# Attention and a two-layer expert on one core: a written table of one line per expert step takes the place of per-step lists

## The chip, the cores and the metric

The kernel runs on one core of one Trainium2 chip. The metric is the device time of one execution in microseconds. The profile is of one execution on the same core, with a record of each instruction, each DMA packet and the TensorE clock that was granted.

The engines are named as in the profile: PE is TensorE's matmul, PEld its weight load, DVE is VectorE, ACT is ScalarE, POOL is GpSimd and SP is SyncE. Each engine carries out its own instructions in the order in which the program issues them, and waits on semaphores for what the other engines give. So the order in which the Python program calls its functions sets the order of every engine's list.

## The reference

Eight batches of eight heads (576 positions, 64 values a head) go through causal attention with a window of 128 and a bias that falls with distance. The result, 4608 tokens of 512 values, goes through a two-layer expert with an ELU.

```
scores = scale * (q @ k^T);  rel = i - j
scores = where((rel >= 0) & (rel < 128), scores - slope[h] * abs(rel), -1e9)
x = (softmax(scores) @ v), heads side by side        # 4608 x 512
h = x @ w_in                                         # 4608 x 2048
g = where(h > 0, h, exp(min(h, 0)) - 1)
out = g @ w_out                                      # 4608 x 512
```

## The kernel before, in words

The expert sets the beat. Its first layer, `hidden`, works in steps: 512 columns of one PSUM bank each, that is four chunks of 128 features by 128 tokens (or eight by 64) in the first 1024 tokens, and two chunks by 256 tokens from token 1024 on (16 steps for each 512 tokens). A step is 16 matmuls (32 where the tokens lie over the end of the ring `xT`, which holds three batches), about 0.87 us on PE. From step 24 on the two banks `hp[0]` and `hp[1]` take turns.

The ELU of a step is a chain over engines. In a "soft" step (the set `SOFT`) ACT does a Relu (L312) and an Exp (L313). In the others ACT does one Exp (L315) and POOL clips it (L316). Then DVE forms `g` from that and the bank (`elu`, L323). The bank is free after that, so step s+2 cannot start on PE before `elu` of step s is done on DVE.

The second layer works for most tokens in units of 256 tokens by a seven-product scheme: `sums` makes four sums of blocks of `g` on DVE (tiles `S1` to `S4`), `product` runs seven products of 8 matmuls each, in the order 1, 2, 6, 5, 7, 3, 4. They take turns in two banks: 1, 6, 7 and 4 in one, 2, 5 and 3 in the other (`op` and `av`, which change roles from unit to unit). Products accumulate on what is in the bank, so ACT copies the bank out between them (tile `U`, or the output tile after product 4: L396, L398), and DVE's `combine` ("C11", "C12", "C22") reads banks and copies and writes the output tile. A bank is written again only when the copy or the combination that reads it is done.

The attention of batches 2 to 7 runs beside this in units of 128 keys, one in four steps. In a unit, `scores` (L225) runs 32-row matmuls that fill four banks, `spa` (two) and `sp[2]`, `sp[3]`. ACT takes the exponential of `spa` in one instruction (L233) and of the two others in one each (L236), DVE weighs the result in two halves (`weigh`, L241), PE multiplies with V (`all_values`, L271, into `spa`), and DVE normalizes in two instructions (L276, L277, tile `xn`). `turn` then sends `xn` transposed into `xT` by a DMA on SP's queue (L285), where `hidden` reads it. The outputs leave on the same SP queue (L417). POOL issues the loads of Q, K and V (L108, L114) in its own list, between the clips.

What comes when is decided by six tables of calls, one list a step: `early`, `HID`, `tasks`, `mid`, `OUT`, `late`. In step s the loop at the end of the kernel issues, in this order: the exponentials of `early`; `hidden(s)` with its two ACT instructions (or ACT and POOL) at once behind the matmuls; `elu` of step s-1; the tasks (weighing, sums, DVE transposes, loads); seven of the products' matmuls, with `all_values`, its normalization and its `turn` behind the second of them; and the rest. A copy to `U` is issued at once behind the eighth matmul of its product. So each step of the seven-product stage has seven product matmuls, and each function issues its whole chain in one piece.

```
for n, (f, a) in enumerate(OUT.get(s, [])):
    if n == 2:
        for g, b in mid.pop(s, []):
            g(*b)
    f(*a)
```

Of the kernel before, what the change touches and what calls it, by code (L numbers as in the profile page):

```python
# [11 lines left out]
ALU = mybir.AluOpType  # L12
# [6 lines left out]
def kernel(  # L19
# [129 lines left out]
    with tc.manual_schedule():  # L149
# [93 lines left out]
        def values(b, i, part, bank=av):  # L243

            m = 128 if i < 4 else 64
            banks = (part, part + 2) if b < 2 else (2 * part, 2 * part + 1)
            parts = [(3, 128, 3), (3, 192, 4)] if i == 4 else [(i, 0, i)] + ([(i - 1, 128, i - 1)] if i else [])
            a = bank[:, 0:4 * (D + 1)].rearrange("p (x h d) -> p x h d", x=2, h=2)
            for x, g in enumerate(banks):
                for h2 in range(2):  # L250
                    for j, (u, c, n) in enumerate(parts):
                        c += 512 * g + 256 * h2
                        nc.tensor.matmul(a[:, x, h2, :], ex_[u][:, c:c + 128], VP[b % 2][:, n, 2 * g + h2, 0:D + 1],
                                         start=j == 0, stop=j == len(parts) - 1)
            if part == 0:
                xnt[b, i] = work.tile([128, 4, 2, D], F16, name="xn", tag="xn", bufs=4)
            o = xnt[b, i][0:m, part::2, :, :] if b < 2 else xnt[b, i][0:m, 2 * part:2 * part + 2, :, :]
            r = work.tile([128, 2, 2], F32, name="rden", tag="rden", bufs=2)
            V.reciprocal(out=r[0:m], in_=a[0:m, :, :, D])
            V.tensor_tensor(out=o, in0=a[0:m, :, :, 0:D], in1=r[0:m].unsqueeze(3).broadcast_to([m, 2, 2, D]),  # L260
                            op=ALU.mult)

        def all_values(b, i):
# [4 lines left out]
            for h in range(H):  # L268
                for j, (u, c, n) in enumerate(parts):
                    c += 256 * h  # L270
                    nc.tensor.matmul(a[:, h // 4, h % 4, :], ex_[u][:, c:c + 128], VP[b % 2][:, n, h, 0:D + 1],  # L271
                                     start=j == 0, stop=j == len(parts) - 1)
            xnt[b, i] = work.tile([128, 4, 2, D], F16, name="xn", tag="xn", bufs=4)
            o = xnt[b, i][0:m].rearrange("p (t g) h d -> p t (g h) d", t=2)
            r = work.tile([128, 2, 4], F32, name="rden", tag="rden8", bufs=2)
            V.reciprocal(out=r[0:m], in_=a[0:m, :, :, D])  # L276
            V.tensor_tensor(out=o, in0=a[0:m, :, :, 0:D], in1=r[0:m].unsqueeze(3).broadcast_to([m, 2, 4, D]),  # L277
                            op=ALU.mult)

        def turn(b, i, copy=None, bank=op):  # L280
# [16 lines left out]
        def hidden(t, c0, w, f0, nf, p, soft):  # L297
            hps[t, c0, f0] = p
            a = (512 * t + c0) % RING
            cuts = [(0, w, a)] if a + w <= RING else [(0, RING - a, a), (RING - a, w, 0)]  # L300
            for l in range(nf):
                fc = f0 + l
                for u0, u1, x0 in cuts:
                    for c in range(4):
                        nc.tensor.matmul(  # L305
                            p[:, l * w + u0:l * w + u1], w_in_sb[:, c, fc * 128:(fc + 1) * 128],
                            xT[:, c, x0:x0 + u1 - u0], start=(c == 0), stop=(c == 3))
            e = es[t, c0, f0] = work.tile([128, 512], F32, name="e", tag="e", bufs=4)
            n = w * nf
            if soft:  # L310

                nc.scalar.activation(e[:, 0:n], p[:, 0:n], AF.Relu, scale=-1.0)  # L312
                nc.scalar.activation(e[:, 0:n], e[:, 0:n], AF.Exp, scale=-1.0)  # L313
                return
            nc.scalar.activation(e[:, 0:n], p[:, 0:n], AF.Exp)  # L315
            nc.gpsimd.tensor_scalar(out=e[:, 0:n], in0=e[:, 0:n], scalar1=1.0, scalar2=0.0,  # L316
                                    op0=ALU.min, op1=ALU.max)

# [67 lines left out]

        def product(n, i, j0=0, j1=8):
            a, b = {1: lambda: (A(n, 0, 0), WB(0, 0)), 2: lambda: (A(n, 0, 1), WB(1, 0)), 3: lambda: (SS[n, 4], WB(1, 1)),
# [3 lines left out]
            for j in range(j0, j1):  # L392
                nc.tensor.matmul(o, a[:, j, :], b[:, j, :], start=j == 0 and i in (1, 2, 5), stop=j == 7,  # L393
                                 skip_group_check=True)
            if j1 == 8 and i in (1, 5, 6, 7):
                nc.scalar.copy(kept(n, i), o)  # L396
            if j1 == 8 and i == 4 and n < 2 * NTB - 1:
                nc.scalar.copy(tile_out(n, 1)[:, 0:256], o)  # L398

        def combine(n, what):  # L400
# [8 lines left out]
            else:  # L409
                add(tile_out(n, 1)[:, 256:512], kept(n, 7), kept(n, 5))  # L410
                if n == 2 * NTB - 2:
# [7 lines left out]
        def last_out(n):  # L419
            for half, queue in enumerate((nc.scalar, nc.sync)):  # L420
# [3 lines left out]
                add(tile_out(n, 1)[:, c], kept(n, 7)[:, c], o)  # L424
                put(n, 1, 128 * half, 128 * half + 128, queue)

        wz = fore[4][:, 0:256]
# [61 lines left out]
        early_expo((hp[1], av), 1, 0)  # L489
        values(0, 0, 0, hp[0])  # L490
        values(0, 0, 1, op)
        early_bias(AB, 128)
        turn(0, 0, V.tensor_copy, hp[0])
        values(0, 1, 0)
        values(0, 1, 1, op)


        early, tasks, mid, late, HID, OUT = {}, {}, {}, {}, {}, {}

# [6 lines left out]
        def after(s, f, *a):  # L506
            late.setdefault(s, []).append((f, a))

        def amid(s, f, *a):
            mid.setdefault(s, []).append((f, a))  # L510

# [49 lines left out]
        at(4, first_expo, 0, 3, 0, 0, 0, 256)  # L561
        at(4, values, 0, 2, 0)
        at(4, values, 0, 2, 1, op)
        at(4, done, 3)
# [4 lines left out]
        at(5, done, 4)  # L569
        at(8, values, 0, 3, 0)  # L570
        at(8, values, 0, 3, 1, sp[3])
        at(10, values, 0, 4, 0)
        at(10, turn, 0, 3, nc.scalar.copy, sp[3])
        at(11, values, 0, 4, 1)
        at(12, turn, 0, 4, nc.scalar.copy, sp[3])
# [16 lines left out]
        for u, a in ((0, 18), (1, 20)):  # L592
            for half in range(2):
# [3 lines left out]
                if (u, half) != (1, 0):  # L597
                    after(a + 2 + half, values, 1, u, half, av if half else sp[2])
        after(22, turn, 1, 0, nc.scalar.copy, av)
        for u, a0, a1 in ((2, 22, 24), (3, 26, 28)):  # L600
            for half, a in enumerate((a0, a1)):
                (after if a == 22 else at)(a, first_scores, 1, u, half, 0)
                (after if a == 22 else at)(a, first_expo, 1, u, half, 0, 0, 256)
                at(a + 1, first_weigh, 1, u, half)
                at(a + 2, values, 1, u, half, av if half else sp[2])
        after(22, values, 1, 1, 0, sp[2])
        at(25, turn, 1, 1, nc.scalar.copy, av)
        at(27, turn, 1, 2, nc.scalar.copy, av)
        at(32, turn, 1, 3, nc.scalar.copy, sp[3])
        at(30, values, 1, 4, 0, sp[2])  # L610
        at(31, values, 1, 4, 1)
        at(32, turn, 1, 4)


        START = [None, None, 31, 48, 66, 83, 100, 117]

        TURN = [None, None, (22, 24, 25, 28), (35, 39, 43, 47)]
        REST = 32, 33, 36, 37
        for b in range(2, B):
            for u in range(4):  # L620
                a = START[b] + 4 * u
                after(a, scores, b, u)
                for g in range(4):
                    before(a + 1 + g // 2, expo, b, u, g)
                at(a + 1, weigh, b, u, 0)
                at(a + 2, weigh, b, u, 1)
                amid(a + 3, all_values, b, u)
                amid(a + 3, turn, b, u)
                if u == 3:
                    at(a + 4, values, b, 4, 0, sp[2])  # L630
                    at(a + 4, values, b, 4, 1, sp[3])
                    at(a + 4, turn, b, 4)
            a = START[b - 1] if b > 2 else 0
# [17 lines left out]
        for n in SEVEN:  # L651
            s = 15 + 8 * n
            ps = (19, 20, 21, 22, 23, 25, 27, 29, 30) if n == 1 else range(s, s + 9)
            if n < 2 * NTB - 1:
                for d, i in ((-1, 1), (1, 2), (3 if n > 1 else -1, 3), (4, 4)):
                    (at_once if n > 2 or n == 1 and i == 2 else at)(ps[d] if d > 0 else ps[0] - 1, sums, n, i)
                if n > 1:
                    after(ps[2], combine, n, "C11")
                after(ps[6], combine, n, "C12")
                (at_once if n > 2 else at)(ps[8], combine, n, "C22")  # L660
                for d in range(8):
                    OUT[ps[d]] = [(product, (n, i, j, j + 1)) for i, j in turns[7 * d:7 * d + 7]]
                if n == 1:
                    OUT[ps[2]].insert(2, (combine, (n, "C11")))
            else:
# [11 lines left out]

        slots = set(HID) | set(OUT) | set(tasks) | set(early)
        for s in range(min(slots), max(slots) + 1):
            for f, a in early.get(s, []):  # L680
                f(*a)
            for step in HID.get(s, []):
                hidden(*step, s in SOFT)
            if s - 1 in HID and s not in (1, 4, 5):
                done(s - 1)
            for f, a in tasks.get(s, []):
                f(*a)
            for n, (f, a) in enumerate(OUT.get(s, [])):
                if n == 2:
                    for g, b in mid.pop(s, []):  # L690
                        g(*b)
                f(*a)
            for f, a in mid.get(s, []):
                f(*a)
# [32 lines left out]
```

## Time and profile before

| what | value |
|---|---|
| runs (3) | median 307.23 us, 306.64 to 308.34 |
| the profiled execution | 307.11 us, of which the span of instructions is 305.2 us |
| granted TensorE clock | 1.00 over the span |
| busy: PE, PEld | 297.6 us, 255.7 us |
| busy: DVE, ACT, POOL | 257.8 us, 241.2 us, 109.1 us |
| step 31 begins, step 148 begins | near 66.5 us, near 289 us |

Busy time is a union of records. PE's records overlap, since matmuls are pipelined, so the sound measure of PE is the distance between the starts of neighbouring matmuls: 109 ns for 256 columns and 56 ns for 128 in this trace. A wait in the table of waits is idle time of an engine just before an instruction, with what ended it.

### The profile page before, as it was taken

To read this page: it belongs to the slowest core of one execution; us is meant where nothing else is said; L and a number is where in the kernel's file an instruction comes from. 1 tells how busy PE (TensorE), PEld (TensorE's weight loads), DVE (VectorE), ACT (ScalarE), POOL (GpSimd) and SP (SyncE) were. 2 spreads that over 40 slices of the span, in tenths; PEclk is the share of its full clock that TensorE was granted. 3 is DMA by queue.
4 is the path that set the end of the run, shared out by engine and by line. 5 is a ranking of instruction groups with operands and counts; after the bars stand their busy time and mean duration, and the time that the engine had idled before them with its cause. 6 is when DMAs were issued, how large, how long until landed. Compare 5 with 4: busy or idle time off the path is not lost.

```text
span 305.2 us, 9832 instructions
## 1 busy us (share of the span) xinstructions
PE 297.6 (98%) x4074; PEld 255.7 (84%) x4074; DVE 257.8 (84%) x499; ACT 241.2 (79%) x445; POOL 109.1 (36%) x163
## 2 busy tenths in 40 slices
PE   7899999999999999999999999999999999999996
PEld 5688876998888889997888888888899888898885
DVE  5746879988989989898989989999998788886783
ACT  5576678869898798877988889778988898968881
POOL 8947958571434234232525061706000001010000
PEclk9999999999999999999999999999999999999999
DMA  9999999999494939292939794999520202030203
GB/s 94 187 199 200 202 185 195 117 125 100 65 141 82 152 34 170 38 179 18 159 45 149 103 116 66 138 133 124 62 88 15 84 17 88 19 97 2 78 13 120
DMA packets 96941, 32.04 MB, mean 105 GB/s; under 512 B 83968, under 2 KB 92800, under 8 KB 96896
## 3 DMA queue, kind: packets, MB, share of 16 engines
q0 software_dynamic: 75920, 18.36, 65.3%
q1 hardware_dynamic: 20832, 12.98, 17.2%
q8 instruction: 32, 0.52, 0.7%
q14 instruction: 13, 0.11, 0.1%
q10 hardware_dynamic: 144, 0.07, 0.1%
HBM read 36.70 MB, written 9.44 MB: 151 GB/s over the span
## 4 chain that ended last, share of the span: by engine, by line
PE 76%; DVE 7%; ACT 7%; DMA 4%; issue 3%; POOL 1%; POOLq 0%; DVEq 0%; ACTq 0%
PE hp L305 34%; PE op L393 13%; PE av L393 12%; PE spa L225 3%; PE spa L271 3%; DVE g L323 2%; DMA VP<-in_v_dram 2%; DMA s<-in_q_dram 2%; ACT EX L236 2%; PE sp L305 2%; PE sp L393 1%; ACT e L315 1%; PE op L329 1%; POOL e L316 1%; PE spa L329 1%
## 5 line engine op out<-in xcount | busy, mean ns | idle before, releaser
L305 PE MATMUL hp<-xT,wi 128*128 128x256 f16 (+3 forms) x1488 | 144.2, 245 | 1.1 <-DVE g L323 0.8
L305 PEld LDWEIGHTS <-wi 128*128 128x128 f16 x1600 | 119.7, 98 | 18.4 <-issue 6.6
L323 DVE SCALAR_TENSOR_TENSOR g<-e,hp 128x512 f16<-128x512 f32 x138 | 93.5, 678 | 21.5 <-ACT e L313 12.4
L316 POOL TENSOR_SCALAR e<-e 128x512 f32<-128x512 f32 x44 | 28.6, 649 | 153.8 <-ACT e L315 150.7
L312 ACT ACTIVATE e<-hp 128x512 f32<-128x512 f32 x98 | 58.6, 598 | 28.1 <-PE hp L305 23.4
L313 ACT ACTIVATE e<-e 128x512 f32<-128x512 f32 x100 | 63.1, 631 | 3.2
L393 PEld LDWEIGHTS <-S 128*128 128x128 f16 x544 | 51.1, 98 | 6.1 <-issue 0.6
L393 PEld LDWEIGHTS <-g 128*128 128x128 f16 x400 | 37.5, 98 | 4.4 <-issue 0.4
L241 DVE TENSOR_TENSOR EX<-EX,TAB 128x1024 f16<-128x1024 f16 x48 | 32.9, 686 | 5.6 <-ACT EX L236 4.0
L114 POOL DMA_DIRECT2D VP<-in_v_dram x40 | 34.3, 871 | 2.0 <-DMA s<-in_k_dram 1.4
L315 ACT ACTIVATE e<-hp 128x512 f32<-128x512 f32 x40 | 24.0, 601 | 10.3 <-PE hp L305 10.3
L393 PE MATMUL op<-T,S 128*128 128x256 f16 x192 | 29.6, 272 | 0.0
L233 ACT ACTIVATE EX<-spa 128x1024 f16<-128x1024 f32 x24 | 24.6, 1026 | 3.7 <-PE spa L225 3.4
L393 PE MATMUL av<-T,S 128*128 128x256 f16 x176 | 27.2, 272 | 0.3 <-DVE ob L354 0.3
L236 ACT ACTIVATE EX<-sp 128x512 f16<-128x512 f32 x48 | 26.0, 597 | 0.0
L354 DVE TENSOR_TENSOR S<-g 128x1024 f16<-128x1024 f16 (+2 forms) x35 | 23.4, 672 | 0.8 <-PE op L393 0.2
L393 PE MATMUL op<-wo,g 128*128 128x256 f16 x128 | 19.7, 273 | 0.0
L393 PE MATMUL av<-wo,g 128*128 128x256 f16 x120 | 18.5, 273 | 0.0
L277 DVE TENSOR_TENSOR xn<-spa,rden 128x512 f16<-128x512 f32 x24 | 16.6, 691 | 0.8
L108 POOL DMA_DIRECT2D st<-in_k_dram x24 | 16.3, 687 | 2.5 <-DMA s<-in_q_dram 2.0
L108 POOL DMA_DIRECT2D st<-in_q_dram x24 | 15.9, 668 | 0.7 <-DMA VP<-in_v_dram 0.7
L225 PE MATMUL sp<-QT,KT 32*128 32x256 f16 (+2 forms) x240 | 15.1, 250 | 0.0
(139 smaller groups left out, 380.8 us busy)
## 6 DMA issues: line engine op xcount, KB each, us to landing
out_dram<-ob SPq DMA_DIRECT2D x32, 256.0 KB, 3.2
VP<-in_v_dram POOLq DMA_DIRECT2D x32, 128.0 KB, 5.9
st<-in_k_dram POOLq DMA_DIRECT2D x24, 144.0 KB, 5.6
st<-in_q_dram POOLq DMA_DIRECT2D x24, 144.0 KB, 6.3
wi<-in_moe_w_in_dram POOLq DMA_DIRECT2D x4, 512.0 KB, 11.9
wo<-in_moe_w_out_dram POOLq DMA_DIRECT2D x4, 512.0 KB, 10.8
out_dram<-ob SPq DMA_DIRECT2D x7, 128.0 KB, 1.7
VP<-in_v_dram POOLq DMA_DIRECT2D x8, 64.0 KB, 5.7
```

The costliest lines, as they stand in the source:

```text
L108: nc.gpsimd.dma_start(st[b][32 * g:32 * g + 32, w, :, :, :, :].rearrange("p h n j d -> p (h n) (j d)"), (q, k)[w][b, 2 * g:2 * g + 2, :, : ...
L114: nc.gpsimd.dma_start(VP[b % 2][0:p, n, :, 0:D], v[b, :, 128 * n:128 * n + p, :].rearrange("h p d -> p h d"))
L233: nc.scalar.activation(unit(b, u)[:, 0:2, :, :], spa.rearrange("p g (h c) -> p g h c", h=2), AF.Exp, scale=0.125)
L236: nc.scalar.activation(unit(b, u)[:, g, :, :], sp[g].rearrange("p (h c) -> p h c", h=2), AF.Exp, scale=0.125)
L241: V.tensor_tensor(out=e, in0=e, in1=TAB[:, int(u == 3), 2 * gp:2 * gp + 2, :, :], op=ALU.mult)
L305: nc.tensor.matmul(p[:, l * w + u0:l * w + u1], w_in_sb[:, c, fc * 128:(fc + 1) * 128], xT[:, c, x0:x0 + u1 - u0], start=(c == 0), stop=(c ...
L312: nc.scalar.activation(e[:, 0:n], p[:, 0:n], AF.Relu, scale=-1.0)
L313: nc.scalar.activation(e[:, 0:n], e[:, 0:n], AF.Exp, scale=-1.0)
L315: nc.scalar.activation(e[:, 0:n], p[:, 0:n], AF.Exp)
L316: nc.gpsimd.tensor_scalar(out=e[:, 0:n], in0=e[:, 0:n], scalar1=1.0, scalar2=0.0, op0=ALU.min, op1=ALU.max)
L323: V.scalar_tensor_tensor(out=gs[t][:, f0:f0 + nf, c0:c0 + w], in0=sh(es.pop((t, c0, f0))), scalar=1.0, in1=sh(hps.pop((t, c0, f0))), op0=A ...
L393: nc.tensor.matmul(o, a[:, j, :], b[:, j, :], start=j == 0 and i in (1, 2, 5), stop=j == 7, skip_group_check=True)
```

## The change

The functions `hidden`, `values` and `all_values` become generators: `hidden` in three parts (matmuls, first ACT instruction, second ACT or POOL instruction), the values in three (matmuls, reciprocal, multiplication). `product` no longer issues its copy; that is `keep`. The addition of "C22" (`lower`) and its output DMA (`put`) are issued apart. Until step 30 the old loop runs, with the generators run through in one piece (`whole`), and again from step 148 on. For steps 31 to 147 a table of 117 lines gives the order of all calls. Each letter takes the next call from a queue of its kind: `h` matmuls of `hidden`, `p` its first ACT instruction, `q` its second (ACT, or POOL in a step that isn't soft), `e` the `elu` of the step before, `o3` three product matmuls, `u` the copy of a product, `k` scores, `x` the exponential of `spa`, `y` and `z` those of `sp[2]` and `sp[3]`, `w` a half of weighing, `v`, `r`, `n` the three parts of the values, `t` the turn, `s1` to `s4` sums, `c1` and `c2` the combinations C11 and C12, `c3` the addition of C22 and `m` its output, `d` a DVE transpose of Q or K, `l` a load. The number of instructions of each kind, their shapes, tiles and buffers are as before.

```
+            yield
             e = es[t, c0, f0] = work.tile([128, 512], F32, name="e", tag="e", bufs=4)
             n = w * nf
             if soft:
-
                 nc.scalar.activation(e[:, 0:n], p[:, 0:n], AF.Relu, scale=-1.0)
+                yield
                 nc.scalar.activation(e[:, 0:n], e[:, 0:n], AF.Exp, scale=-1.0)
...
-            if j1 == 8 and i in (1, 5, 6, 7):
-                nc.scalar.copy(kept(n, i), o)
-            if j1 == 8 and i == 4 and n < 2 * NTB - 1:
-                nc.scalar.copy(tile_out(n, 1)[:, 0:256], o)
+            if j1 == 8 and copy:
+                keep(n, i)
+
+        def keep(n, i):
+            if i in (1, 5, 6, 7):
+                nc.scalar.copy(kept(n, i), place(n, i))
+            elif i == 4 and n < 2 * NTB - 1:
+                nc.scalar.copy(tile_out(n, 1)[:, 0:256], place(n, i))
+
+        def lower(n):
+            add(tile_out(n, 1)[:, 256:512], kept(n, 7), kept(n, 5))
...
+        def whole(f, *a):
+            for _ in f(*a):
+                pass
...
-            for u in range(4):
-                a = START[b] + 4 * u
-                after(a, scores, b, u)
-                for g in range(4):
-                    before(a + 1 + g // 2, expo, b, u, g)
-                at(a + 1, weigh, b, u, 0)
-                at(a + 2, weigh, b, u, 1)
-                amid(a + 3, all_values, b, u)
-                amid(a + 3, turn, b, u)
...
+        SCRIPT = """
+o1 h o2 p o1 k l q o1 e o1 v y l t d o1
+            h x r n e o1 t o1 p o4 s2 u
+            h q w o2 e o2 z o4 d p o1
+            h w q c1 o2 p v e o4 q o1 r
+            h s3 u n o2 p o2 e o1 t o1 u k s4 q o1
...
+            h w q y e o4 z o2 c3 o2 p o2 w m
+            h q c1 v u e p o4 s3 o1 q o1
+            h r n o2 p o1 e o1 t o1 k q s4 u
+            h e x d o3 p o2 w o1
+            h y q z l o1 e o1 u o3 p o1 w o2
...
+            h u q c3 v m e t o3 u o2 r o1 p s4 o3
+            h n q o1 e t o1 p k d u q
+            h x l e o2 p o1 w o4 z o1 q
+            h c2 y l e o2 p o2 w l o4 q
...
+            h m t u w q o4 e v u p o2 r o3 n o1 q o1
+            h t e o3 u k p c3 q
+            h x l e o2 p o2 w o3 y o1 q
...
+            h r n q c1 o2 n p o3 e o1 t o2 q k d u
+            h x e s4 o2 p o1
+            h w z d q o5 u o2 e o1 p o4 y o2 q o1
+            h u w o1 e o1 p o3 v c3
+            h q r n l o2 e p o1 t o2 l o2 s3 q k l u c2
+            h x e m l o3 p
+            h w l q s1 l o2 z o2 e o3 y o5 p o1 w
+            h q s2 v u e p o4 c1 o1 q
...
+            h q c1 e o2 p o3 c3 o2
+            h q m u e o2 p o5 q u
+        """
...
+        for s in range(16 * NTB + 9):
+            if s in script:
+                for x in script[s]:
+                    x, n = ("o", int(x[1:])) if x[0] == "o" else (x, 1)
+                    for _ in range(n):
+                        f, a = next(queues[x])
+                        f(*a)
+                continue
```

In the cut above the first five lines are steps 31 to 35; the next groups are steps 41 to 45, 51 to 54, 59 to 61, 66 to 73 and 146 to 147.

## The prediction

> **What bounds the kernel now.** First the page's busy row, then the windows of 10 us, to see which engine has no room in the stage that the table covers (from near 66.5 us to near 289 us).
>
> ```profile
> PE 297.6 (98%) x4074; PEld 255.7 (84%) x4074; DVE 257.8 (84%) x499; ACT 241.2 (79%) x445; POOL 109.1 (36%) x163
> ...
> 140.00:150.00 10.00, 9.69 (x106) 8.18 (x104) 8.52 (x16) 8.14 (x17) 6.10 (x8) 1.00 0.63 70
> 150.00:160.00 10.00, 9.91 (x125) 8.47 (x123) 8.51 (x17) 8.46 (x17) 1.52 (x3) 1.00 0.80 88
> ...
> 280.00:290.00 10.00, 10.00 (x94) 8.97 (x92) 6.71 (x12) 8.26 (x16) 0.00 (x0) 1.00 0.17 60
> ```
>
> PE is the bound: in most windows its records leave no gap, at a granted clock of 1.00. From 270 to 300 us the attention is over, matmuls follow each other every 109 ns (256 columns), and PE can do no better. DVE and ACT have 10 to 20% of room each, so their sums set nothing; their order can.
>
> Then the waits of PE's weight loads between 66.5 and 270 us, where the idle time of a row is in its third field:
>
> ```profile
> PEld L305 <- issue: 6.2, 27, 0.5
> PEld L225 <- issue: 5.0, 24, 0.2
> PEld L393 <- issue: 0.6, 2, 0.4
> PEld L305 <- DMA xT<-xn: 0.2, 1, 0.2
> ```
>
> Together 12.0 us, but most of it is not a wait. The 24 score units each show 0.21 us before their first load, and the 18 of them that end in 256 columns 0.22 us after their last, whatever was ready: a cost of going to 32-row matmuls and back. The change keeps these units, so 24 x 0.21 + 18 x 0.22 = 9.0 us of the 12 stay.
>
> What is left I took from start times in the timeline: each matmul's distance from the one before, less the usual distance for that neighbour (109 ns, 56 ns, 202 ns behind scores). From 66.5 us on there are 21 late starts of over 40 ns, which sum to 3.7 us, and 1.0 us in smaller ones: **4.7 us is all that an order can win there**. Of the 3.7, some 3.1 stand before a `hidden`, which waits for its bank (or, once, for `xT`); 0.6 stand before or among products, which wait for a sum or a combination. The largest in the steady stage, in the order of its chain:
>
> ```profile
> 141.07 1.09 ACT L236 ACTIVATE EX<-sp 128x512 f16<-128x512 f32 x2
> ...
> 142.04 0.61 ACT L315 ACTIVATE e<-hp 128x512 f32<-128x512 f32 x1
> ...
> 142.81 0.61 POOL L316 TENSOR_SCALAR e<-e 128x512 f32<-128x512 f32 x1 [10.06 <-ACT e L315]
> ...
> 143.45 0.69 DVE L323 SCALAR_TENSOR_TENSOR g<-e,hp 128x512 f16<-128x512 f32 x1 [0.57 <-POOL e L316]
> ...
> 143.61 0.27 PE L393 MATMUL op<-T,g 128*128 128x256 f16 x1
> ...
> 144.19 1.03 PE L305 MATMUL hp<-xT,wi 128*128 128x256 f16 x8 [0.31 <-DVE g L323]
> ```
>
> Two exponentials (1.09 us) stand on ACT ahead of the ELU's own, then POOL, then DVE, and PE starts step 70 at 144.19 where 143.61 + 0.11 was possible: 0.47 us late. The same pattern gives the lateness at 159.85 (0.25) and 243.60 (0.34).
>
> **A rule weighed.** The Trainium skill, page "Perfetto Trace Analysis", section "Identifying the Most-Contended Engine", says that matmul occupancy tells little of PE's headroom and that weight-load occupancy does. By that, 84% would leave 16% of 305 us, 49 us. The row at 280 to 290 us speaks against it: with nothing waited for, weight loads still read 8.97 of 10, since a load of 98 ns sits in each 109 ns. The 64-column values and the scores lower it further. So I take 4.7 us from start times, not 49.
>
> **The change part by part.** No instruction is added or taken away, so on every engine the work sums as before; only lists change. I counted DVE's list of before from its records and the table's from its letters: at each step they differ by at most a few instructions.
>
> (1) Products move between steps. Before, each step has 7 (0.76 us). In the table the step in which ACT has the exponentials of `sp[2]` and `sp[3]` gets mostly 8 to 13 and the step of `x` mostly 3 to 6. In steps 67 to 70, around the chain above, it is 3, 15, 5, 7. The exponentials are parted too: in step 68 `y` (0.55 us) goes behind `p`, so the chain to POOL starts 0.55 us sooner in ACT's list, and 15 products (1.64 us) give it cover. This takes the 0.47. Over all `hidden` starts I count 2.4 of the 3.1 us as won: the rest is in steps 53 to 62, where `xT` is late instead (4).
>
> (2) Sums and combinations. At 75.06 us a product waits for C11, queued behind a weighing and a transpose (0.42 us). The table has C11 and sums at a distance of 0.3 to several us of PE work from their use, plus the matmuls that they lie beside. I count the 0.6 us as won, and half of the 1.0 us in small starts. Gains: 2.4 + 0.6 + 0.5 = 3.5 us.
>
> (3) Copies. Before, a copy (0.36 us) stands on ACT behind its product's last matmul, and its bank is wanted again 8 products and at least one `hidden` later (0.87 + 0.87 us). The table puts `u` up to 2.1 us of PE work behind the product. Adding up PE work between `u` and the bank's next use, 10 of some 70 have less than 0.45 us, 14 more less than 0.7. I worked out steps 71 to 73. ACT, from the start of step 71: x 1.03, p 0.60, q 0.63, z and y 1.09, p 0.60, q 0.63, u 0.36, with gaps of 0.02, ends near 5.1 us. PE: 0.87 + 3 x 0.109 = 1.20; 0.87 + 13 x 0.109 = 2.29; 0.87 and the values 0.5; at 4.86 the first matmul of product 6 wants the bank of that copy. It waits about 0.3 us, and behind it on PE wait four products and step 74. In the trace of before, the same steps (146.5 to 151.9 us) have no late start. Bounds for all copies: 0 (ACT runs ahead) to 10 x 0.46 = 4.6 us (all ten in full). I take 0.6, nearer to nothing: many of the ten stand right behind an `h`, beside whose 0.87 us they run.
>
> (4) `turn`, outputs, loads. `n` goes one step later for many tiles, and so does `t` behind it on SP's list. For the tile that step 54 waits for, `t` is in step 52 with 2.45 us of PE work to go; for step 62 2.67; for step 46 3.98. The DMA issues of before, in the windows 110 to 113.5 us and 100 to 108 us, show what a transpose takes (last field, us to landing):
>
> ```profile
> xT<-xn SPq DMA_TRANSPOSE x1, 2.4
> ...
> out_dram<-ob SPq DMA_DIRECT2D x1, 256.0 KB, 4.6
> VP<-in_v_dram POOLq DMA_DIRECT2D x1, 128.0 KB, 5.6
> xT<-xn SPq DMA_TRANSPOSE x2, 4.8
> ```
>
> Alone it takes 2.4 us, beside loads and an output 4.8. In step 51 the table issues an output (`m`) and a transpose on SP's list 1 to 2 us ahead of the tight one. Here a second rule speaks against the change: the skill's page "DMA: Bandwidth & Descriptors", section "Queues, rings and completion order", says that SP owns one ring on each DMA engine and that descriptors are taken in ring order. By the rule the tight transpose stands behind 256 KB, and with 4.8 - 2.4 it costs up to 2.4 us at step 54 alone. By the row of 2.4 it costs nothing. No load lies close there in the table, so I take 0.5 us for the three steps, with 0 and 5 as ends. The loads go in clusters on POOL as before (clips of POOL hold them back); each is issued at least 8.9 us of PE work before its transpose on DVE, against 5.6 to 6.3 us to landing in the page's rows, so they cost nothing; with that cover gone DVE would stand for the rest of one landing, up to 6 us once. `m` apart from `c3` keeps SP from standing still, which nobody waits for.
>
> Sum: 3.5 - 0.6 - 0.5 = 2.4 us. The profiled execution took 307.11 us (span 305.2), 0.1 below the median of the runs; 307.1 - 2.4 = **304.7 us**.
>
> **The rivals.** (a) Traded: the new order gives late starts of its own, near 0.2 us in about 20 places, as step 73 suggests and as the smallest late starts of before are (0.1 to 0.25 us). Then 3.5 is met by 3 us or more: 306.6 us. It also covers the case that the order hardly differs where it matters. For it: DVE's list is nearly the same. Against it: the steps' product counts follow ACT's load closely. (b) Slower: ACT's list. With its copies shifted behind `p`, `q`, `y`, ACT decides when PE may write a bank. If ACT runs 0.3 us behind what the table allows for, the 24 copies with less than 0.7 us cost 24 x 0.3 = 7.2 us against 4.7 won: 309.6 us. It is slower than before from about 0.2 us a copy (24 x 0.2 = 4.8). ACT's 84% in this stage (170 of 203.5 us) speaks against a lasting lag.
>
> **How the numbers follow.** A change under 0.5% (1.5 us) can hardly be told from none, with runs that spread over 1.7 us. Main case 0.63: 304.7, its own range 302.8 to 305.8. Traded 0.26: 306.6. Slower 0.11: 309.6. The floor is 307.1 - 4.7 = 302.4, which needs all late starts gone. The range of 302.8 to 307.6 holds the main case and most of (a). Faster by over 0.5% means under 305.6: the main case nearly whole, 0.64; slower by over 0.5% 0.11; between them 0.25.
>
> **What would show it.** Right: in the stage from 66.5 us no `hidden` starts more than 0.3 us late behind a product; the start at step 70 comes without a wait on DVE's `g`; PE's sum of busy time hardly changes while the span falls. Wrong by (4): waits "L305 <- DMA xT<-xn" of over 0.5 us at steps 46, 54 or 62. Wrong by (3) or (b): waits of products (L393) on ACT's `U`, and lines of `L396` in the chain that ended last. If the span falls by more than 4.7 us, the cost of score units was not fixed, and my base is wrong.

## The result and the profile after

The changed kernel takes 304.41 us (median of 8 runs, 303.97 to 306.68) against 307.18 us (8 runs beside it), a ratio of 0.9914 with a 95% interval of 0.9885 to 0.9942. Two later sets of runs of the same file gave 0.9939 (0.9915 to 0.9963) and 0.9932 (0.9909 to 0.9955). The forecast was 304.7 us. The medians of the three sets differ by 2.77, 1.75 and 2.24 us.

The page's busy row and three windows after, which answer to those of before:

```profile
PE 296.7 (98%) x4074; PEld 255.8 (84%) x4074; DVE 255.3 (84%) x499; ACT 238.2 (79%) x445; POOL 109.4 (36%) x163
...
140.00:150.00 10.00, 10.00 (x121) 8.68 (x119) 8.84 (x17) 8.19 (x17) 6.15 (x8) 1.00 0.83 103
150.00:160.00 10.00, 10.00 (x141) 8.52 (x139) 9.00 (x17) 7.71 (x16) 3.79 (x6) 1.00 0.89 73
278.00:288.00 10.00, 10.00 (x94) 8.97 (x93) 7.53 (x13) 8.29 (x17) 0.00 (x0) 1.00 0.09 34
```

Behind a window and its length stand PE's busy time and that of its weight loads (8.68, 8.52, 8.97). The instruction counts are the same, and PE is still the bound; what was open for PE in the windows of 140 to 160 us (9.69 and 9.91 of 10) is closed. The stretch without attention reads 8.97 for weight loads, as before.

How long the table's stage takes is best read from two starts on DVE, `elu` of step 30 and of step 147 (the kernel before, then the changed one; columns: start, duration, engine, line):

```profile
68.74 0.67 DVE L323 SCALAR_TENSOR_TENSOR g<-e,hp 128x512 f16<-128x512 f32 x1
...
292.82 0.69 DVE L323 SCALAR_TENSOR_TENSOR g<-e,hp 128x512 f16<-128x512 f32 x1 [0.35 <-ACT e L313]
```

```profile
67.91 0.67 DVE L332 SCALAR_TENSOR_TENSOR g<-e,hp 128x512 f16<-128x512 f32 x1
...
290.24 0.69 DVE L332 SCALAR_TENSOR_TENSOR g<-e,hp 128x512 f16<-128x512 f32 x1 [0.95 <-ACT e L320]
```

292.82 - 68.74 = 224.08 us before, 290.24 - 67.91 = 222.33 after. Below, "stage" means this difference. It came out at 224.02 in a second profile of before, and at 222.28 and 221.92 in two more of after: profiles of one kernel lie within 0.1 us before and 0.4 us after, where the time of a run moves by 1 to 2 us. The stage explains 1.75 us of the 2.5 us between the first two spans. The other 0.8 us lie ahead of step 30, where the order of calls is as before (last section).

The chain of steps 68 to 70 in the changed kernel:

```profile
139.78 0.60 ACT L322 ACTIVATE e<-hp 128x512 f32<-128x512 f32 x1
...
140.27 0.60 ACT L236 ACTIVATE EX<-sp 128x512 f16<-128x512 f32 x1
...
140.54 0.61 POOL L324 TENSOR_SCALAR e<-e 128x512 f32<-128x512 f32 x1 [9.13 <-ACT e L322]
...
141.62 0.67 DVE L332 SCALAR_TENSOR_TENSOR g<-e,hp 128x512 f16<-128x512 f32 x1
...
142.35 0.49 PE L311 MATMUL hp<-xT,wi 128*128 128x256 f16 x3
```

The exponential of `sp[2]` now comes behind the ELU's own (140.27 behind 139.78), POOL is done at 141.15, and DVE takes `g` without a wait ahead of it (the line carries no bracket). The bank is free at 142.29, and PE, kept busy by products and values, starts step 70 only 0.05 us late, where it was 0.47.

By the prediction's measure (start to start, less the usual distance) the late starts of the stage are:

| | before | after |
|---|---|---|
| `hidden`, waiting for its bank | 3.09 us with `xT` (18 places over 40 ns) | 1.05 us |
| `hidden`, waiting for `xT` | in the line above | 0.59 us (step 46: 0.16, step 102: 0.43) |
| products | 0.58 us | none |
| values (after: waiting for a weighing in step 38) | 0.05 us | 0.20 us |
| late starts of under 40 ns each | 1.42 us | 1.55 us |
| sum | 5.14 us | 3.39 us |

The difference of the sums, 1.75 us, is that of the stages to about 0.1 us: the start of step 31 (0.32 us late before, 0.20 after) is counted, though it lies ahead of the stage's first mark. PE's waits in the stage of the changed kernel, in the profile's words (us in total, times, longest):

```profile
PEld L225 <- issue: 4.8, 23, 0.2
PEld L311 <- issue: 3.3, 14, 0.5
PEld L402 <- issue: 2.2, 10, 0.2
PEld L311 <- DMA xT<-xn: 0.3, 1, 0.3
PEld L274 <- DVE EX L241: 0.2, 1, 0.2
```

Most of it is again the price of the score units, 0.2 us each, which both kernels pay. Since the table puts products, not only a `hidden`, behind scores, that price now stands in the rows of L402 (10 times 0.2) as well. The row by itself looks like a new wait for products; it is none.

### The profile page after: what moved, and what is told of

Read it like the earlier page. It is cut to its first block, busy times and chain, and to the rows that moved or that the text cites. A ratio compares the mean times of both kernels' runs of the same rounds, so it can differ in the third digit from the quotient of the medians.

```text
span 302.7 us, 9837 instructions
## 1 busy us (share of the span) xinstructions
PE 296.7 (98%) x4074; PEld 255.8 (84%) x4074; DVE 255.3 (84%) x499; ACT 238.2 (79%) x445; POOL 109.4 (36%) x163
## 4 chain that ended last, share of the span: by engine, by line
PE 83%; DMA 7%; DVE 5%; POOL 2%; ACT 1%; issue 1%; POOLq 0%; DVEq 0%; ACTq 0%
PE hp L311 36%; PE op L402 15%; PE av L402 14%; DMA VP<-in_v_dram 5%; PE spa L225 4%; PE spa L274 3%; DMA st<-in_k_dram 2%; PE op L451 2%; DVE g L332 2%; PE sp L402 1%; DVE xn L262 1%; PE sp L253 1%; ACT e L322 1%; POOL e L324 1%; PE sp L311 1%
## 5 line engine op out<-in xcount | busy, mean ns | idle before, releaser
L320 ACT ACTIVATE e<-e 128x512 f32<-128x512 f32 x100 | 63.6, 636 | 2.2
L402 PEld LDWEIGHTS <-S 128*128 128x128 f16 x544 | 51.0, 98 | 6.6 <-issue 1.1
L402 PEld LDWEIGHTS <-g 128*128 128x128 f16 x400 | 37.0, 98 | 5.4 <-issue 1.5
L402 PE MATMUL op<-T,S 128*128 128x256 f16 x192 | 29.5, 273 | 0.0
L402 PE MATMUL av<-T,S 128*128 128x256 f16 x176 | 27.0, 273 | 0.0
L236 ACT ACTIVATE EX<-sp 128x512 f16<-128x512 f32 x48 | 27.0, 603 | 0.0
L402 PE MATMUL op<-wo,g 128*128 128x256 f16 x128 | 20.4, 273 | 0.0
L402 PE MATMUL av<-wo,g 128*128 128x256 f16 x120 | 19.7, 273 | 0.0
```

Source lines behind the costliest of these rows:

```text
L236: nc.scalar.activation(unit(b, u)[:, g, :, :], sp[g].rearrange("p (h c) -> p h c", h=2), AF.Exp, scale=0.125)
```

## The experiments

Only the table was edited. A table gives one list to each engine, and POOL's list is the same in both kernels. So the change is four lists: PE, ACT, DVE, SP. The first three edits take one list back at a time (those of DVE and SP together).

**The changed kernel again.**

> The changed kernel once more, unedited, for a second profile and more times. Theory 1 (the gain lies in the late starts of the stage from step 31): 304.4 us; late starts from step 31 on near 1.9 us in those over 40 ns, as in the first profile (3.7 before). Rival S (0.8 us of the 2.5 us between the two profiles lies before step 31, in the landing of the first loads of Q and K, and is chance): the start of step 31 moves by up to 0.8 us between profiles of one kernel, and the times lie nearer 305.2.

Measured: 305.23 us, stage 222.28, late starts over 40 ns 1.80 us in the same nine places. `elu` of step 30 began at 70.18 us where it was 67.91: the time ahead of the stage moves by 2.3 us, the stage by 0.05. Theory 1 held for the late starts and missed the time. Rival S held for the time; what it put at up to 0.8 us was 2.3. So the stage gain is no chance, and the 0.8 us ahead of it may well be.

**PE's list as before** (steps 67 and 68 of the edit):

```
-            h x e s4 o2 p o1
-            h w z d q o5 u o2 e o1 p o4 y o2 q o1
+            h x p o1 w z d q o5 u o1
+            h o1 e o1 p o4 y o1 q
```

> The table with PE's list as before (seven product matmuls a step, values and scores where they were), all other engines' lists as after. Theory 1 (products moved to the steps in which ACT has the exponentials win the hidden starts): most of the gain is lost, 306.3 to 307.5 us, with late starts before hidden of 2.5 us or more. Rival A (ACT's order, p ahead of y, does it): 304.4 to 305.2. Rival D (DVE's order): 304.4 to 305.2.

**ACT's list as before** (step 68):

```
-            h w z d q o5 u o2 e o1 p o4 y o2 q o1
+            h w d q o5 u o2 e o5 y z p o2 q o1
```

> The table with ACT's list as before from step 32 on (y and z side by side ahead of p, each copy behind p and q of its step), all other lists as after. Theory 1: a part is lost, 304.8 to 305.6 us, since the products' places still cover the chain. Rival A (ACT's order does it): 306.5 to 307.5. Rival D: 304.4.

**The lists of DVE and SP as before** (steps 33 and 34):

```
-            h q w o2 e o2 z o4 d p o1
-            h w q c1 o2 p v e o4 q o1 r
+            h q w d s2 o2 e o2 z o4 p o1
+            h w d q c1 o2 p v e o4 q o1
```

> The table with the lists of DVE and SP as before (elu first in each step, normalization and turn behind it, output with its addition), the lists of PE and ACT as after. Theory 1: within 0.5 us of the changed kernel, 304.4 to 304.9 us. Rival D (DVE's order does it): 306.5 to 307.5. The transposes are issued in the old order, but behind the new PE order; waits of hidden for xT of 0.3 us in sum are expected by all.

Measured: 309.01, 309.91 and 309.54 us, with ratios to before of 1.007 (1.0043 to 1.0098), 1.0095 (1.0069 to 1.0121) and 1.0066 (1.0041 to 1.0091); stages 226.43, 225.94 and 226.28. Every expected time fell. None gives back "its part": each costs 3.6 to 4.1 us of stage and ends slower than before, where the whole change won 1.75. One old list (or the two of DVE and SP) among new ones is worse than all old ones. Part of what is lost there are a few large waits of 0.45 to 1.1 us, where two orders meet; it is no measure of what a list is worth. With PE's old list, products wait 1.3 us in sum; with ACT's, a single product waits 1.07 us for a copy that stands behind two ELUs on ACT:

```profile
261.94 0.63 ACT L320 ACTIVATE e<-e 128x512 f32<-128x512 f32 x1
...
262.48 0.35 ACT L409 COPY U<-op 128x256 f32<-128x256 f32 x1
...
262.88 0.27 PE L402 MATMUL op<-T,S 128*128 128x256 f16 x1 [0.90 <-ACT U L409]
```

So a new theory M: the lists are one plan, and no single list carries the gain. The next edit tries it from the other side, with the new list of PE alone.

**The order of before, with only PE's list new** (step 68 as above in the ACT edit, DVE's edit besides).

> The order of before on ACT, DVE and SP (from step 32 on), with PE's list as after: step (1) of the prediction by itself. Stage means the time from the start of elu of step 30 to that of step 147: 224.1 us before, 222.3 after. Theory M (the four lists are one plan, and each alone is worse than none): 225 to 227. Prediction's step (1) taken alone (moved products give the chain its cover): 222.5 to 223.5.

Measured: stage 227.81, 3.7 us longer than before (one run, 310.46 us). That speaks for theory M, though it is 0.8 us above its range, and the expectation of step (1) fell. The moved products win nothing by themselves: PE comes to products whose sums and copies the other engines still make in their old order (1.7 us of late starts there, 4.1 us at `hidden`).

**Copies directly behind their products** (steps 68 and 69):

```
-            h w z d q o5 u o2 e o1 p o4 y o2 q o1
-            h u w o1 e o1 p o3 v c3
+            h w z d q o3 u o4 e o1 p o3 u o1 y o2 q o1
+            h w o1 e o1 p o3 v c3
```

> The table with each copy u moved up to stand directly behind the eighth matmul of its product, as before; all else as after. If the copies' late places cost PE anything by late bank release (prediction's step 3): stage shorter than 222.3 us by up to 0.6. If their late places serve to let p and q go first on ACT: stage longer, 222.8 to 224, with hidden starts late behind DVE's g. If neither: 222.3 within 0.1.

Measured: stage 227.92, 5.6 us longer; one run, 310.85 us. It is the second expectation, and above its range. This is no return to ACT's list of before: there a step's `p` and `q` stand ahead of its copies, here `u` comes ahead of them. Late starts rise to 7.2 us, 5.9 of them at `hidden`; about 1.4 us at step 102 is a wait for `xT` that the new times brought. Some 2.3 us more, which the changed kernel does not have, come within 4.5 us after ACT has stood at a copy. One case is shown (kernel with early copies):

```profile
224.84 1.06 PE L311 MATMUL hp<-xT,wi 128*128 128x128 f16 x16
...
226.15 0.37 ACT L411 COPY ob<-av 128x256 f32<-128x256 f32 x1 [0.96 <-PE av L402]
...
226.42 0.60 ACT L318 ACTIVATE e<-hp 128x512 f32<-128x512 f32 x1
...
227.05 0.63 ACT L320 ACTIVATE e<-e 128x512 f32<-128x512 f32 x1
...
227.72 0.69 DVE L332 SCALAR_TENSOR_TENSOR g<-e,hp 128x512 f16<-128x512 f32 x1 [0.74 <-ACT e L320]
...
228.46 0.33 PE L311 MATMUL hp<-xT,wi 128*128 128x128 f16 x3
```

ACT stands for 0.96 us at a copy whose product PE has not finished. The matmuls of the ELU behind it end at 225.90, and it starts at 226.42. DVE then waits 0.74 us for that ELU, and PE's next `hidden` starts 0.26 us late. ACT's waits for products at copies (to `U` and the output tile) are 0.4 us in the kernel before, 3.7 us in the changed one and 10.7 us here. What makes the rest of the 5.6 us was not traced.

**The loads of batch 7 behind the clips** (steps 96, 102, 103):

```
-            h l x e l o1 s2 o1 p o5 d u o2 q o1
+            h x e o1 s2 o1 p o5 d u o2 q o1
...
-            h q c2 z l e o2 p o3 w l o3 q
-            h s1 l e o2 p v l o2 r o1 u
+            h q c2 z e l l l o2 p o3 w o3 q
+            h s1 e l l o2 p v o2 r o1 u
```

> The table with the last four loads of Q of batch 7 moved on POOL's list from before the clips of steps 100 and 101 to behind them, and the five of V spread behind these. If the late start of step 102 (0.43 and 0.38 us in two profiles) is the transpose that lands beside a cluster of loads: that transpose takes near 2.4 us in place of 4.6, the late start goes, stage 221.9. If it is the bank or the weighing that the profile names: stage 222.3, late start stays.

Measured: stage 221.92, and the late start of step 102 is gone; one run, 305.38 us. It looks like a clean hit, but it isn't one: the third profile of the unedited kernel has the same stage, 221.92, and no late start there either. The two views are of the DMA issues around 200 us, first in the first profile of the changed kernel, then in its third (last field: us to landing):

```profile
xT<-xn SPq DMA_TRANSPOSE x1, 4.6
```

```profile
xT<-xn SPq DMA_TRANSPOSE x1, 2.4
```

The same transpose beside the same loads takes 4.6 us in one execution and 2.4 in another. That step 102 waits for this landing is shown: it came at 204.61 in the first profile and PE starts at 204.75; in the second the same two times are 206.81 and 206.95. (The profile names a weighing that ended 0.07 us before the start.) That the cluster of loads makes it slow is not shown.

**Products moved ahead of late hidden starts** (steps 33, 34, 101, 102):

```
-            h q w o2 e o2 z o4 d p o1
-            h w q c1 o2 p v e o4 q o1 r
+            h q w o2 e o2 z o4 d p o3
+            h w q c1 p v e o4 q o1 r
...
-            h e o2 p o1 w o4 y
-            h q c2 z l e o2 p o3 w l o3 q
+            h e o2 p o1 w o4 y o4
+            h q c2 z l e p o1 w l o3 q
```

> The changed table with product matmuls moved from behind a late hidden to ahead of it (two each at steps 31, 34, 38, 46 and 63, four at step 102), and one weighing ahead of the DVE transpose in step 38. If PE only lacked something to do while it waited: 1.2 to 1.6 us of the 1.85 us in late starts are won, stage 220.8 to 221.2, time near 303.2. If each moved product makes the next hidden late instead: stage 222.0 to 222.5, time as the changed kernel's.

Measured: 304.69 us, ratio 0.9925 (0.9898 to 0.9952), stage 221.56. Against 221.9 to 222.3 of the changed kernel that is 0.4 to 0.8 us, a quarter to a half of what was expected, and in neither range: part of the late starts came back a step later (0.34 us at step 39, where there were 0.18 and 0.20 in step 38). The times of the runs don't tell it from the changed kernel.

**The kernel before again.**

> The kernel before, unedited, for a second profile. Theory 1: the stage from elu of step 30 to that of step 147 takes 224.1 us within 0.1, as in its first profile, against 222.3 in both profiles of the changed kernel. Rival S: it lies elsewhere by 0.5 us or more, and the stage gain of 1.8 us is partly chance.

Measured: stage 224.02, late starts over 40 ns 3.67 us in the same 21 places; one run, 307.61 us. Theory 1 held.

**The pair of exponentials side by side** (step 68):

```
-            h w z d q o5 u o2 e o1 p o4 y o2 q o1
+            h w z y d q o5 u o2 e o1 p o6 q o1
```

> The changed table with the exponentials y and z side by side again in the 7 units where p stood between them; all else as after. Prediction's step (1), second half (a parted pair lets the chain to POOL and DVE start 0.55 us sooner): late hidden starts come back in those units, stage 222.8 to 224. If the moved products alone give the cover: 222.3 within 0.2.

Measured: stage 224.65; one run, 307.65 us. Of the 2.3 to 2.7 us by which that is longer, 1.02 us is one wait at step 31, where the moved exponential reads a bank that a turn of batch 1 is about to write; that belongs to the edit, not to the question. Without it the stage is 223.63. Step 102 had no late start here, so it is fair to compare with the third profile's 221.92, and 1.7 us stay. Cut into stretches of nine steps, they lie in steps 66 to 93 and 111 to 129, where pairs were joined. One of these places, first in the changed kernel, then with the pair joined:

```profile
238.04 0.63 ACT L320 ACTIVATE e<-e 128x512 f32<-128x512 f32 x1
...
238.84 0.68 DVE L332 SCALAR_TENSOR_TENSOR g<-e,hp 128x512 f16<-128x512 f32 x1
239.10 0.59 ACT L236 ACTIVATE EX<-sp 128x512 f16<-128x512 f32 x1
...
239.57 0.49 PE L311 MATMUL hp<-xT,wi 128*128 128x256 f16 x3
```

```profile
240.10 1.08 ACT L236 ACTIVATE EX<-sp 128x512 f16<-128x512 f32 x2
...
241.06 0.64 ACT L320 ACTIVATE e<-e 128x512 f32<-128x512 f32 x1
...
241.73 0.69 DVE L332 SCALAR_TENSOR_TENSOR g<-e,hp 128x512 f16<-128x512 f32 x1 [0.28 <-ACT e L320]
...
242.47 0.60 PE L311 MATMUL hp<-xT,wi 128*128 128x256 f16 x4 [0.39 <-DVE g L332]
```

Joined, both exponentials stand ahead of the ELU's second instruction (L320), DVE waits for it, and PE starts 0.56 us late where it was 0.18. So parting these pairs is worth some 1.7 us in this table, by one profile of the edit.

**Both repairs, and step 120** (steps 119 and 120; the loads and step 34 as above):

```
-            h y s1 q w o2 p o3 e o2 z o2 c3
-            h u w q m o1 e v p o4 s2 u o2 q
+            h y s1 q w o2 p o3 e o2 z o2 c3 u o2
+            h w q m e v p o3 s2 u o2 q
```

> The table of loads_late, with one product moved ahead of hidden at step 31 and two each at steps 34, 46, 63 and 120 (there with its copy). If the remaining late starts are PE time that a product can fill: 0.6 us less than loads_late's 221.9, stage 221.3, time 1.0 us below the changed kernel's in the same rounds. If they come back a step later: 221.9 or more.

> The changed kernel, unedited, on the same chip and in the same rounds as tuned2. Stage 222.3 us within 0.1 in a third profile; time 304.4 to 305.3.

Measured: 304.90 us over six executions (ratio 0.9918, 0.9889 to 0.9946) and, for the unedited kernel beside it, 304.99 us (0.9932, 0.9909 to 0.9955). The only profile of the repaired kernel is of a seventh execution, of 1690 us, so its stage is not known. The 1.0 us of time that was expected did not come. For the unedited kernel the time held and the stage did not: 221.92, not 222.3. No version was shown to beat the changed kernel.

## Why the prediction was right

The base held: what was won came out of late starts, and their sums before and after differ by the stage's difference to about 0.1 us. What could be won, put at 4.7 us, came to 5.14 us when the small starts were counted in full, and not to the 49 us that weight-load occupancy would allow; 1.75 us of it were won. By its steps:

(1) Hidden starts: 2.4 of 3.1 us forecast, 3.09 - 1.05 = 2.0 us measured at the banks. The mechanism was half right. That parted exponentials let the chain start sooner is shown (1.7 us in this table). But the step spoke of moved products as of something that gives cover by itself, and that fell: with PE's new list alone the stage is 3.7 us longer than before.

(2) Products: 0.6 us forecast, 0.58 us measured. The half of the small starts (0.5 us) was not won; they went from 1.42 to 1.55 us. I had put them at 1.0 us, and as waits. Values in step 38 now wait 0.2 us for a weighing, which no step had.

(3) Copies: a cost of 0.6 us forecast, none found. No product waits for its bank in any of the profiles of the changed kernel, and the wait of 0.3 us at step 73 is absent. The slack that I added up took `u` as if it ran when PE had got that far in the table; it can run sooner, and beside the matmuls. The step also left out what a copy does to ACT, which stands still at one that comes too early: moving the copies up in this table costs 5.6 us. That their late places win anything against the kernel before is not shown, for there ACT waited only 0.4 us at copies.

(4) Transposes: 0.5 us forecast for steps 46, 54 and 62, measured 0.16 us at step 46, none at 54 and 62, and 0.43, 0.38 and 0 us at step 102, which I had not named. The size was right in two of three profiles, the place mostly wrong. By the Trainium skill's rule that descriptors are taken in ring order ("DMA: Bandwidth & Descriptors", "Queues, rings and completion order"), the tight transpose of step 52 stands behind an output and another transpose. It took 2.4 us to landing, but that is no test of the rule: when it was issued, that output had only 0.1 us to go. The transpose of step 51 is a test. It was issued 0.4 us behind the same output, on the same queue (first profile of the changed kernel, last field: us to landing):

```profile
out_dram<-ob SPq DMA_DIRECT2D x1, 256.0 KB, 2.1
xT<-xn SPq DMA_TRANSPOSE x1, 2.3
```

It landed 0.6 us after the output, which fits ring order, and yet took no longer than one alone (2.4). So the up to 2.4 us that the prediction drew from the rule did not come, and the row of 2.4 us was the right one to go by.

The gains that were too high (1, small starts) and the cost that was too high (3) cancel in part: 2.4 us forecast, 1.7 to 2.2 us of stage measured. That the first set of runs came within 0.3 us of the forecast is in part luck, since of its 2.77 us up to 1 us is not the stage's.

Rival (a), traded, did not occur: there are nine late starts over 40 ns and not some 20, though a few of 0.2 us are new. For it stood that DVE's list is nearly the same; but with the old lists of DVE and SP the stage is 3.95 us longer, so those lists matter. Rival (b), ACT's copies deciding, did not occur in this table, but in the one with ACT's old list it did (1.07 us at one product). Of the signs that the prediction named, one failed: step 102 starts 0.43 and 0.38 us late behind a product in two profiles, and it waits for `xT`.

What stays open: how the 1.75 us divide among the lists. The runs show that they don't add up, so the question may have no answer; two or three new lists among old ones, other than those shown, were not tried.

## What to carry to other kernels

Where engines run in order and PE is 98% busy, count what an order can win from start-to-start distances before believing any busy share. Move work in whole plans: here PE's list from the better order, set among old ones, cost twice what the whole order won. On an engine with spare time, too, look at what stands too early in its list (here a copy that waits for its product), since all behind it wait with it; copies that stood late held no product up in this table.

## What the runs showed of the hardware

The time of an execution moves far more ahead of the stage than in it. Two profiles of one file, the changed kernel's first and second, in the window of 10 to 20 us (the column before the last two is the granted clock):

```profile
10.00:20.00 10.00, 8.99 (x199) 7.58 (x200) 6.05 (x14) 6.33 (x11) 6.69 (x16) 1.00 1.35 193
```

```profile
10.00:20.00 10.00, 9.15 (x197) 7.64 (x196) 6.42 (x17) 6.25 (x10) 7.03 (x16) 0.87 1.39 198
```

In the second the clock was granted in part for a few microseconds, PE waited 1.2 us for Q to land at 8.37 us, which the first does not show, and step 30's `elu` came 2.3 us later. The first profile of before has a like wait (1.1 us at 7.93 us) and the full clock. Up to step 30 all these kernels issue the same code, and over the profiles step 30's `elu` starts anywhere from 67.8 to 70.2 us, with 68.74 and 69.27 for the kernel before. So this is chance of an execution and no part of the change, and it can be larger than the change itself. The stage, by contrast, repeats to 0.1 us apart from one transpose, which took 4.6, 4.5 and 2.4 us in three executions of one program.
